# Five PSUM banks in one group, and due offsets by attention unit

## The chip, the cores and the metric

The kernel runs on one core of a Trainium2 chip, as one launch. The metric is the device time in microseconds (us). Before the change the median of three runs is 717.65 us (716.26 to 718.03).

## The reference, cut to what matters

Three stages follow one another on 3072 tokens of 384 features. The first is a linear attention with decay, 4 batches of 768 steps and 8 heads of 48. The second is a feed-forward layer of width 2048. The third is a layer of eight experts of width 1024, of which one is picked for each token.

```python
for t in range(S):                                   # attention, per batch and head
    y[:, :, t] = r_t @ (state + outer(u * k_t, v_t))
    state = w * state + outer(k_t, v_t)
h = x @ w_in                                         # first feed-forward layer
g = where(h >= 1, h, where(h <= -1, 0, (h + 1)**2 / 4))
x = g @ w_out
e = argmax(normed(x) @ normed(emb).T / tau)          # experts
out = gate * (relu(x @ w1[e]) @ w2[e])
```

## The kernel before, in words

Attention is cut into 24 units of 128 tokens, six to a batch. A unit u has three jobs on TensorE, which the planner calls `s0`, `s1` and `s2`:

- `s0` (`s0_pe`, L598 or L606, tiles `psa`) makes the scores of all heads. It fills two PSUM banks at once. VectorE reads them into the SBUF tile `at` (`s0_ev`, L618, or L621 and L625).
- `s1` (`s1_pe`, L672, tile `psy`) makes the outputs, from the scores and from the state that the unit before has left. It fills one bank, which ScalarE and VectorE split into a high and a low float32r part (`xh`, L730, and `xl`, L736).
- `s2` (`s2_pe`, L697 to L706, tile `pskv`) makes the unit's sum of key times value for the state. It fills one bank, which ScalarE or VectorE reads.

The first layer takes blocks of 512 tokens against 16 slices of 128 columns of `w_in`. A step k is one slice: `h` (`m1_h`, nine matmuls into one bank, tile `psh`), on ScalarE `relu`, `over` and `sqr` (L817, L821, L824), on VectorE `max` (L827), on ScalarE `gh` (L831), on GpSimd `gl` (L836), and on TensorE `o` (L858, L859) and `og` (L861), which add the step to three accumulators `acc0` to `acc2`. The bank of `h` comes free after `max`. The experts use `h2` or, for blocks 1 to 5, four tasks `sm` (`sm_pe`), each with one bank.

PSUM has eight banks here: three accumulators, two with the tag `h` and three with the tag `att`. Tag `h` serves the first layer's products, the experts' products, the first two of the four `sm` banks and the diagonal sums of the first four units (`dg_pe`). Tag `att` serves `psa`, `psy`, `pskv`, the other two `sm` banks, the fourth output of the experts and some small tiles.

The order of the work is not written by hand. `Schedule.add` collects tasks with an engine, a duration, dependences, buffers and a due time; `Schedule.run` plays the engines forward. On each engine it takes, among the tasks that can start first, the one due first, and a task whose buffer tag has no free slot has to wait. The slot it finds is the bank the code then uses (`spot`). The due time is moved by the table `SHIFT`, which is looked up under the task's kind (`s0`), its item (`u7`) and both together (`s0_u7`). Before `first_o`, the first task that opens the accumulators, the loop that emits the code fills planned gaps of TensorE with matmuls into a dummy tile (`keep_warm`, L743, tile `wu`). Each engine, and the DMA queue of SyncE, gets its instructions in the planned order.

Of the kernel before, what the change touches and what calls it, by code (L numbers as in the profile page):

```python
# [21 lines left out]
B, H, S, D = 4, 8, 768, 48  # L22
# [204 lines left out]
def d_pe(n):  # L227
    return n / 2300 + 0.011


SHIFT = {"": 62, "az": 0.25, "b0": 147.25, "b2": -0.25, "b4": 29, "b5": 16.75, "dd": 39.25, "dp": -2.25, "dv": 15.5,
# [15 lines left out]
         -6.25, "le0": 7.75, "le1": 46, "le2": -8.75, "lka": -1.5, "lkl": -25.5, "lkm": 6.75, "look": 6, "max":  # L247
# [5 lines left out]
         "smc1": 60.25, "sqa": 2.25, "sqr": 95.25, "sqs": 22.5, "swd": 70.5, "swl": 27, "sws0": 25.5, "sws1": -10.25,  # L253
# [7 lines left out]
         "wb2": 29.75, "wb3": -386.25, "whi": -13, "whp": -29.75, "wkc": 27, "wkd": 28.75, "wkr": -10.5, "wl": 47,  # L261
         "wlo": -0.25, "wlp": -88.75, "wp1": 7.5, "wp2": 3, "wp3": -29, "x1ld": -13, "x1st": -35.75, "x2h": 120.5,
         "x2l": 15.25, "x2ld": -25.5, "xth0": 88.75, "xth1": -7, "xtl0": -3, "xtl1": -35.25, "xts0": -50, "xts1":
         -61.25, "xts2": -25.25, "xts3": -16.25}
U_DVE, U_PE, W_DVE = 4.7, 3.5, 4.0
# [5 lines left out]
def fused_kernel(ctx, tc, att, wcol, wrow, ub, ucol, win, wout, emb, tau, w1, w2, out):  # L271
# [28 lines left out]
    now, turn = {}, {}  # L300

    def spot(tag, bufs):
        if now.get(tag):
            return f"{tag}{now[tag].pop(0)}"
        assert "all" not in now, tag
        turn[tag] = turn.get(tag, -1) + 1
        return f"{tag}{turn[tag] % bufs}"

# [174 lines left out]
    n = 1  # L483
# [73 lines left out]
    def dg_pe(u):  # L557
        s = st[u]
        s["dgp"] = psum("h", [128, H], "psdg", 2)
        for p in range(NP):  # L560
            nc.tensor.matmul(s["dgp"][:, 2 * p:2 * p + 2], lhsT=s["kr"][:, p, :], rhs=uw[:, p, :], start=True, stop=True)
# [245 lines left out]
    def m1_h(m, f, c0, n, f0=0, f1=NF):  # L807
        xh, xl = xT[m]
        hp = psum("h", [128, 512], "psh", 2)[:, :n]
        for kk in range(KD):  # L810
            prod3(hp, win_h[:, kk, f * 128:(f + 1) * 128], win_l[:, kk, f * 128:(f + 1) * 128],
                  xh[:, kk, c0:c0 + n], xl[:, kk, c0:c0 + n], kk == 0, kk == KD - 1)
        return hp
# [327 lines left out]
    def sm_pe(b, q, i, ws):  # L1141

        p = psum("h" if i < 2 else "att", [128, 2, 256], f"psm{i}", 2 if i < 2 else 3)
        mq[b, q, i] = p
# [44 lines left out]
    def m2_hpe(b, f, ws):  # L1189
        n = blocks2[b][1]  # L1190
        _, xh, xl = x2[b][:3]
        hp = psum("h", [128, 512], "psh2", 2)[:, :n]
        for kk in range(KD):
            prod3(hp, ws[0][:, kk, f * 128:(f + 1) * 128], ws[1][:, kk, f * 128:(f + 1) * 128],
                  xh[:, kk, :n], xl[:, kk, :n], kk == 0, kk == KD - 1)
        return hp
# [51 lines left out]
    def m2_store(b, i, o):  # L1248
# [3 lines left out]

    sch = Schedule({"att": 3, "h": 2, "acc0": 1, "acc1": 1, "acc2": 1, "ld": 4, "attn": 2, "x1": 2, "xh": 2, "xl": 2,
                    "a": 2, "gh": 3, "gl": 3, "ru": 1, "dg": 2, "dv": 1, "at0": 1, "at1": 1, "state": 2, "kk": 2, "hw": 2, "gate": 1},
# [40 lines left out]
    def go(k):  # L1295
        return [seq[k]] if seq.get(k) else []
    for m in range(len(blocks1)):
        xbuf[m] = Buf("xh"), Buf("xl")
    for u in range(NU):
# [31 lines left out]
        if u < RAMP:  # L1331
            dpb = Buf("h")
            kr = add("kr", f"u{u}", "Pool", 1.5, lambda u=u: prep_kr(u), [rk], due - 6.5, alloc=[rub], use=[ab])
# [85 lines left out]
    for k, s in enumerate(steps):  # L1419
        m, f, c0, n, f0, f1 = s  # L1420
        hb, ab, ghb, glb = Buf("h"), Buf("a"), Buf("gh"), Buf("gl")
        toks = [u for u in range(NU) if unit_blk[u][0] == m and c0 <= unit_blk[u][1] < c0 + n]
        h = add("h", f"k{k}", "PE", 9 * d_pe(n), run(("h", k), m1_h, *s[:4]), [w_ready["in", f // 2], prev_h] + [lo_of[u] for u in toks],
                T[k], alloc=[hb], use=list(xbuf[m]))
        prev_h = h_of[k] = h
        r = add("relu", f"k{k}", "ACT", 0.65, lambda k=k, n=n: got.update({("a", k): m1_relu(got["h", k], n)}), [h], T[k], alloc=[ab], use=[hb])
        q = add("over", f"k{k}", "ACT", 0.65, lambda k=k: m1_over(got["a", k]), [r], T[k], use=[ab])
# [138 lines left out]
    for k, (b, f) in enumerate(steps2):  # L1566
# [40 lines left out]
        if b in SB:  # L1607
            if f % 2 == 0:
                q = f // 2
                mb = [Buf(x) for x in ("h", "h", "att", "att")]  # L1610
                gb2 = [(Buf("gh"), Buf("gl")) for _ in range(2)]
# [23 lines left out]
        if b not in SB:  # L1635
            hb, ghb, glb = Buf("h"), Buf("gh"), Buf("gl")
            h = add("h2", f"b{b}", "PE", 9 * d_pe(n), lambda b=b, f=f: got.update({("h2", b, f): m2_hpe(b, f, ws)}),
                    his + los + [w2_ready[f // 2], prev_h], due, alloc=[hb], use=[xhb, xlb])
            prev_h = h
            if f in (0, 5):  # L1640
                p2_go[f // 5] = h
            g = add("gh2", f"b{b}", "ACT", d_act(n), lambda b=b, f=f: got.update({("g2", b, f): m2_gh(b, f, got["h2", b, f])}), [h], due, alloc=[ghb], use=[hb])
            g2 = add("gl2", f"b{b}", "DVE", d_dve(n), lambda b=b, f=f: m2_gl(b, f, got["h2", b, f], got["g2", b, f]), [g], due, alloc=[glb], use=[hb, ghb])
# [271 lines left out]
```

## Time and profile before

| | |
|---|---|
| median of three runs | 717.65 us |
| the profiled execution's own time | 718.3 us |
| its span, first to last instruction | 716.6 us |
| PE busy (TensorE) | 705.6 us, 98% |
| DVE busy (VectorE) | 444.2 us, 62% |
| ACT busy (ScalarE) | 413.4 us, 58% |
| POOL busy (GpSimd) | 299.7 us, 42% |
| granted TensorE clock | 0.999 of full speed |

The trace is one execution on the chip. A timeline row gives the start, the time covered, the engine, the line of the kernel, the operation, output and inputs, the number of instructions merged and, in brackets, how long the engine sat idle before the row and what ended that. Matmuls overlap in the pipe: one of 128x512 is shown with 0.40 us and the next begins 0.23 us after it, so the distance between two starts is what it costs. The busy time of PE therefore covers short gaps too.

### The profile page before, as it was taken

The page shows a single profiled execution, that of the slowest core. Times are in us where ns is not written, and L with a number is a line of the kernel's source. Part 1 is how long each engine was busy: PE and PEld are TensorE (multiplying, and loading weights), DVE is VectorE, ACT ScalarE, POOL GpSimd, SP SyncE. Part 2 cuts the span into 40 slices and gives each one's busy share as a digit, 9 for nine tenths or more (in the row PEclk, how much of TensorE's full clock was granted, in tenths as well). Part 3 has the DMA queues.
Part 4 walks back from the last instruction along what each step waited for, and adds up shares of the span by engine and source line. Part 5 has one row for each costly group of instructions (what it writes and reads, how often), then busy time and mean ns, then how long its engine had stood idle before and what let it go on. Part 6 is the DMA issues. An engine that isn't in the chain of part 4 may idle for free.

```text
span 716.6 us, 14161 instructions
## 1 busy us (share of the span) xinstructions
PE 705.6 (98%) x5727; PEld 596.4 (83%) x5727; DVE 444.2 (62%) x824; ACT 413.4 (58%) x738; POOL 299.7 (42%) x247
## 2 busy tenths in 40 slices
PE   8999999999999999999999999999999999999997
PEld 7788887877777888777778878888789999999996
DVE  7988787777777614925274444321657886848952
ACT  3366667674546555745667868776536455437431
POOL 5599965645646633453233313334452113012000
PEclk9999999999999999999999999999999999999999
DMA  8666535222513402510046545300412111102011
GB/s 301 218 224 213 182 132 183 90 97 88 194 67 131 140 12 71 202 31 1 1 143 238 192 138 166 95 0 1 132 45 67 54 57 45 46 22 68 1 45 48
DMA packets 26136, 74.93 MB, mean 105 GB/s; under 512 B 2505, under 2 KB 9682, under 8 KB 26066
## 3 DMA queue, kind: packets, MB, share of 16 engines
q1 hardware_dynamic: 25778, 73.59, 30.4%
q8 instruction: 46, 0.75, 0.4%
q10 hardware_dynamic: 288, 0.39, 0.1%
q14 instruction: 24, 0.20, 0.1%
HBM read 62.74 MB, written 11.01 MB: 103 GB/s over the span
## 4 chain that ended last, share of the span: by engine, by line
PE 82%; DVE 9%; ACT 3%; issue 2%; POOL 2%; DMA 1%; DVEq 0%; ACTq 0%; SPq 0%; POOLq 0%
PE psh L323 9%; PE psh L325 8%; PE psh L324 8%; PE acc L861 8%; PE acc L858 8%; PE acc L859 8%; PE o L1228 5%; PE o L1225 4%; PE o L1226 4%; PE psm L323 3%; PE psm L324 3%; PE psm L325 3%; PE psy L672 3%; DVE a L827 1%; PE psa L606 1%
## 5 line engine op out<-in xcount | busy, mean ns | idle before, releaser
L836 POOL TENSOR_TENSOR gl<-a,gh 128x512 fp32r<-128x512 f32 (+1 forms) x98 | 139.4, 1425 | 183.3 <-ACT gh L831 175.4
L827 DVE TENSOR_TENSOR a<-psh,a 128x512 f32<-128x512 f32 (+1 forms) x98 | 66.3, 677 | 138.4 <-ACT a L824 136.9
L323 PE MATMUL psh<-xh,win_h 128*128 128x512 f32 (+1 forms) x294 | 117.6, 400 | 0.8 <-DVE a L827 0.8
L817 ACT ACTIVATE a<-psh,half 128x512 f32<-128x512 f32 (+1 forms) x98 | 66.2, 675 | 88.5 <-PE psh L325 68.4
L858 PE MATMUL acc<-gh,wout_h 128*128 128x512 f32 (+1 forms) x294 | 115.6, 394 | 0.2 <-ACT gh L831 0.2
L325 PE MATMUL psh<-xh,win_l 128*128 128x512 f32 (+1 forms) x294 | 114.9, 391 | 0.0
L324 PE MATMUL psh<-xl,win_h 128*128 128x512 f32 (+1 forms) x294 | 114.8, 391 | 0.0
L859 PE MATMUL acc<-gh,wout_l 128*128 128x512 f32 (+1 forms) x294 | 114.5, 391 | 0.0
L831 ACT ACTIVATE gh<-a 128x512 fp32r<-128x512 f32 (+1 forms) x98 | 60.5, 619 | 49.3 <-DVE a L827 45.4
L861 PE MATMUL acc<-gl,wout_h 128*128 128x512 f32 (+1 forms) x294 | 82.1, 392 | 1.1 <-POOL gl L836 1.1
L1185 DVE TENSOR_TENSOR sc<-sc,psm 128x256 f32<-128x256 f32 x160 | 59.2, 416 | 17.3 <-ACT sc L1175 11.3
L323 PEld LDWEIGHTS psh<-xh,win_h 128*128 128x128 f32 x294 | 55.2, 188 | 16.5 <-DVE a L827 2.7
L858 PEld LDWEIGHTS acc<-gh,wout_h 128*128 128x128 f32 x294 | 55.2, 188 | 14.0 <-ACT gh L831 0.6
L861 PEld LDWEIGHTS acc<-gl,wout_h 128*128 128x128 f32 x294 | 54.0, 188 | 14.9 <-POOL gl L836 2.3
L325 PEld LDWEIGHTS psh<-xh,win_l 128*128 128x128 f32 x294 | 55.2, 188 | 12.8
L859 PEld LDWEIGHTS acc<-gh,wout_l 128*128 128x128 f32 x294 | 55.3, 188 | 12.4
L1225 PE MATMUL o<-w2h,gh 128*128 128x384 f32 x192 | 64.9, 338 | 0.0
L324 PEld LDWEIGHTS psh<-xl,win_h 128*128 128x128 f32 x294 | 55.3, 188 | 11.3
L1226 PE MATMUL o<-w2l,gh 128*128 128x384 f32 x192 | 64.4, 336 | 0.0
L821 ACT ACTIVATE a<-a 128x512 f32<-128x512 f32 (+1 forms) x98 | 60.8, 621 | 2.4
L824 ACT ACTIVATE a<-a 128x512 f32<-128x512 f32 (+1 forms) x98 | 60.6, 618 | 2.0
L1200 ACT ACTIVATE gh<-sc 128x512 fp32r<-128x512 f32 x40 | 24.5, 627 | 43.2 <-DVE sc L1185 30.7
(216 smaller groups left out, 1372.2 us busy)
## 6 DMA issues: line engine op xcount, KB each, us to landing
att<-att SPq DMA_DIRECT2D x22, 736.0 KB, 4.6
w<-wout SPq DMA_DIRECT2D x16, 768.0 KB, 4.4
w<-win SPq DMA_DIRECT2D x16, 768.0 KB, 5.3
attn<-att SPq DMA_DIRECT2D x20, 384.0 KB, 3.5
x1d<-x SPq DMA_DIRECT2D x6, 768.0 KB, 4.7
x1f<-x1d SPq DMA_DIRECT2D x6, 768.0 KB, 4.8
out<-o SPq DMA_DIRECT2D x10, 384.0 KB, 2.4
hw<-w SPq DMA_DIRECT2D x8, 384.0 KB, 3.6
```

The source lines that it names most:

```text
L323: nc.tensor.matmul(o, lhsT=sh, rhs=mh, start=first, stop=False, skip_group_check=True)
L324: nc.tensor.matmul(o, lhsT=sh, rhs=ml, start=False, stop=False, skip_group_check=True)
L325: nc.tensor.matmul(o, lhsT=sl, rhs=mh, start=False, stop=last, skip_group_check=True)
L817: nc.scalar.activation(out=a, in_=hp, func=AF.Relu, bias=half[:, 0:1], scale=0.5)
L821: nc.scalar.activation(out=a, in_=a, func=AF.Relu, bias=1.0, scale=-1.0)
L827: nc.vector.tensor_tensor(out=a if out is None else out, in0=hp, in1=a, op=ALU.max)
L836: (eng or nc.gpsimd).tensor_tensor(out=gl, in0=a, in1=gh.bitcast(F32), op=ALU.subtract)
L858: nc.tensor.matmul(o, lhsT=wh, rhs=gh, start=(f == f0 and c0 == 0), stop=False, skip_group_check=True)
L859: nc.tensor.matmul(o, lhsT=wl, rhs=gh, start=False, stop=False, skip_group_check=True)
L861: nc.tensor.matmul(o, lhsT=wh, rhs=gl, start=False, stop=(f == f1 - 1), skip_group_check=True)
L1225: nc.tensor.matmul(o, lhsT=gh[:, c], rhs=ws[2][:, f, :], start=(f == 0), stop=False, skip_group_check=True)
L1226: nc.tensor.matmul(o, lhsT=gh[:, c], rhs=ws[3][:, f, :], start=False, stop=False, skip_group_check=True)
```

## The change

The two banks `h` and the three banks `att` become one group of five with the tag `att`; the planner gives a bank of it to whichever task asks. `relu` tasks get a fixed order, each after the one before. The table `SHIFT` is replaced as a whole; the new one also has entries that move `s0`, `s1` and `s2` of single units. `spot` counts its turns by tag and number of buffers, for the code outside the plan. Nothing is computed otherwise, and no tile changes its size.

```diff
-SHIFT = {"": 62, "az": 0.25, "b0": 147.25, "b2": -0.25, "b4": 29, "b5": 16.75, "dd": 39.25, "dp": -2.25, "dv": 15.5,
...
+SHIFT = {"": -54, "az": -68.5, "b0": -144.75, "b1": -92.5, "b2": -72.5, "b3": -73.75, "b4": -0.5, "b5": 11.5, "dd":
...
+         230, "rt0": -6.25, "rt1": 50, "rt2": 44.25, "ru0": -16.25, "ru1": 159.75, "s0_u0": 15.25, "s0_u1": 177.75,
+         "s0_u10": 17.75, "s0_u11": 81.5, "s0_u12": -1.75, "s0_u13": 76.5, "s0_u14": 0.75, "s0_u15": -24.75,
...
@@ spot
-        turn[tag] = turn.get(tag, -1) + 1
-        return f"{tag}{turn[tag] % bufs}"
+        turn[tag, bufs] = turn.get((tag, bufs), -1) + 1
+        return f"{tag}{turn[tag, bufs] % bufs + (2 if (tag, bufs) == ('att', 3) else 0)}"
@@ dg_pe
-        s["dgp"] = psum("h", [128, H], "psdg", 2)
+        s["dgp"] = psum("att", [128, H], "psdg", 2)
@@ m1_h
-        hp = psum("h", [128, 512], "psh", 2)[:, :n]
+        hp = psum("att", [128, 512], "psh", 2)[:, :n]
@@ sm_pe
-        p = psum("h" if i < 2 else "att", [128, 2, 256], f"psm{i}", 2 if i < 2 else 3)
+        p = psum("att", [128, 2, 256], f"psm{i}", 3)
@@ m2_hpe
-        hp = psum("h", [128, 512], "psh2", 2)[:, :n]
+        hp = psum("att", [128, 512], "psh2", 2)[:, :n]
@@ fused_kernel
-    sch = Schedule({"att": 3, "h": 2, "acc0": 1, "acc1": 1, "acc2": 1, "ld": 4, "attn": 2, "x1": 2, "xh": 2, "xl": 2,
+    sch = Schedule({"att": 5, "acc0": 1, "acc1": 1, "acc2": 1, "ld": 4, "attn": 2, "x1": 2, "xh": 2, "xl": 2,
...
-            dpb = Buf("h")
+            dpb = Buf("att")
...
-        hb, ab, ghb, glb = Buf("h"), Buf("a"), Buf("gh"), Buf("gl")
+        hb, ab, ghb, glb = Buf("att"), Buf("a"), Buf("gh"), Buf("gl")
...
-        r = add("relu", f"k{k}", "ACT", 0.65, lambda k=k, n=n: got.update({("a", k): m1_relu(got["h", k], n)}), [h], T[k], alloc=[ab], use=[hb])
+        r = add("relu", f"k{k}", "ACT", 0.65, lambda k=k, n=n: got.update({("a", k): m1_relu(got["h", k], n)}), [h], T[k], alloc=[ab], use=[hb],
+                after=go("relu"))
+        seq["relu"] = r
...
-                mb = [Buf(x) for x in ("h", "h", "att", "att")]
+                mb = [Buf("att") for _ in range(4)]
...
-            hb, ghb, glb = Buf("h"), Buf("gh"), Buf("gl")
+            hb, ghb, glb = Buf("att"), Buf("gh"), Buf("gl")
```

## Rows read from the trace of the kernel before

**Rows 1.** The page: busy time and share by engine; then PE by slices.

```profile
PE 705.6 (98%) x5727; PEld 596.4 (83%) x5727; DVE 444.2 (62%) x824; ACT 413.4 (58%) x738; POOL 299.7 (42%) x247
PE   8999999999999999999999999999999999999997
```

**Rows 2.** Waits of PE: line, releaser, us in total, times, longest.

```profile
PE wu L743 <- POOL mask L468: 2.0, 1, 2.0
PE acc L861 <- POOL gl L836: 1.1, 2, 0.9
PE psh L323 <- DVE a L827: 0.8, 3, 0.4
PE o L1228 <- DVE gl L1205: 0.6, 1, 0.6
PE psa L598 <- DVE at L618: 0.6, 1, 0.6
```

**Rows 3.** Windows: length, busy by engine (instructions), clock, DMA share, GB/s.

```profile
2.02:36.10 34.08, 33.35 (x471) 27.40 (x471) 30.34 (x61) 9.97 (x30) 18.12 (x21) 1.00 0.79 275
60.00:100.00 40.00, 40.00 (x222) 32.22 (x221) 33.48 (x35) 28.35 (x48) 34.24 (x23) 1.00 0.52 178
150.00:200.00 50.00, 48.42 (x636) 37.67 (x635) 37.39 (x82) 28.89 (x59) 29.00 (x23) 1.00 0.40 133
```

**Rows 4.** Timeline of PE about a trip with scores alone, the first.

```profile
204.27 0.40 PE L324 MATMUL psh<-xl,win_h 128*128 128x512 f32 x1
204.50 0.39 PE L325 MATMUL psh<-xh,win_l 128*128 128x512 f32 x1
204.82 0.90 PE L606 MATMUL psa<-att 64*64 64x128 f32 x32
205.65 0.50 PE L858 MATMUL acc<-gh,wout_h 128*128 128x512 f32 x1
205.98 0.39 PE L859 MATMUL acc<-gh,wout_l 128*128 128x512 f32 x1
```

**Rows 5.** Timeline of PE: the last of the trips with scores alone.

```profile
370.53 0.90 PE L606 MATMUL psa<-att 64*64 64x128 f32 x32
```

**Rows 6.** Timeline of PE: a state sum and scores in one trip.

```profile
150.45 0.54 PE L706 MATMUL pskv<-att,kk 128*32 128x48 f32 x32
150.92 0.90 PE L606 MATMUL psa<-att 64*64 64x128 f32 x32
151.76 0.50 PE L323 MATMUL psh<-xh,win_h 128*128 128x512 f32 x1
```

**Rows 7.** Timeline of PE: a state sum that ends a trip.

```profile
282.55 0.52 PE L706 MATMUL pskv<-att,kk 128*32 128x48 f32 x32
283.01 0.50 PE L323 MATMUL psh<-xh,win_h 128*128 128x512 f32 x1
```

**Rows 8.** Timeline of PE: a product that waits for its bank.

```profile
180.16 0.40 PE L325 MATMUL psh<-xh,win_l 128*128 128x512 f32 x1
180.97 0.50 PE L323 MATMUL psh<-xh,win_h 128*128 128x512 f32 x1 [0.41 <-DVE a L827]
```

**Rows 9.** Lines of PE from 2 to 36.1 us: busy, mean ns, idle before.

```profile
L743 PE MATMUL wu<-mask,ident 128*128 128x128 f32 x44 | 7.2, 329 | 2.0 <-POOL mask L468 2.0
```

**Rows 10.** Timeline of the start, PE about 30 us.

```profile
28.70 1.83 PE L743 MATMUL wu<-mask,ident 128*128 128x128 f32 x14
30.45 0.48 PE L598 MATMUL psa<-att 64*128 64x128 f32 x2
...
31.53 1.16 PE L598 MATMUL psa<-att 64*128 64x128 f32 x14 [0.59 <-DVE at L618]
```

**Rows 11.** Timeline: a unit's scores filled, and the second bank of them read.

```profile
39.35 1.16 PE L598 MATMUL psa<-att 64*128 64x128 f32 x16
...
44.19 0.68 DVE L618 TENSOR_TENSOR at<-psa,mask 128x512 f32<-128x512 f32 x1
```

**Rows 12.** Waits of DVE from 0 to 60 us.

```profile
DVE att L523 <- DMA att<-att: 2.8, 3, 1.4
```

More of the change, by code (lines that the diff above doesn't have):

```diff
@@ L228, in d_pe @@
     return n / 2300 + 0.011
-SHIFT = {"": 62, "az": 0.25, "b0": 147.25, "b2": -0.25, "b4": 29, "b5": 16.75, "dd": 39.25, "dp": -2.25, "dv": 15.5,
[15 rows of a table removed]
-         -6.25, "le0": 7.75, "le1": 46, "le2": -8.75, "lka": -1.5, "lkl": -25.5, "lkm": 6.75, "look": 6, "max":
[5 rows of a table removed]
-         "smc1": 60.25, "sqa": 2.25, "sqr": 95.25, "sqs": 22.5, "swd": 70.5, "swl": 27, "sws0": 25.5, "sws1": -10.25,
[7 rows of a table removed]
[L261 to L264, printed above, removed]
+SHIFT = {"": -54, "az": -68.5, "b0": -144.75, "b1": -92.5, "b2": -72.5, "b3": -73.75, "b4": -0.5, "b5": 11.5, "dd":
[15 rows of a table added]
+         64.25, "le0": 2.5, "le1": 18.5, "le2": -32, "lka": -6.75, "lkl": 0.5, "lkm": -54.5, "look": -78.25, "max":
[14 rows of a table added]
+         "sqa": -18, "sqr": -189.5, "sqs": 24.75, "swd": -6.5, "swh": 8.25, "swl": 46.75, "sws0": -20.25, "sws1":
[11 rows of a table added]
 U_DVE, U_PE, W_DVE = 4.7, 3.5, 4.0
```

65 rows, old and new, of the table SHIFT are left out of this document.

## The prediction

> **What bounds the kernel now.** First the page's busy times and slices: PE is busy 705.6 of 716.6 us and no slice but the first and the last is below nine tenths [rows 1]. No other engine has over 62%. So time can only go where PE does something that is not work, and the view to read next is the waits of PE [rows 2]: 2.0 us before its first matmul, 1.1 for `gl` of GpSimd, 0.8 in three waits of `psh` for `max` on VectorE, 0.6 for `gl` in the experts, 0.6 in one wait of `psa`. Two of these five are waits for a PSUM bank: `max` is the last reader of an `h` bank, and L618 the reader of a `psa` bank. Together 1.4 us. The rest of PE's waste is not idle time and is read from the distances between starts in the timeline. It has two kinds: edges, where PE leaves the long matmuls for small attention ones and comes back, and the dummy matmuls `wu` of the start.
>
> **An edge's price.** In a run of long products the starts are 0.23 us apart. Before a trip the last one takes 204.50 to 204.82 = 0.32, and after it the first takes 205.65 to 205.98 = 0.33 [rows 4]. So a trip costs 0.09 + 0.10 = 0.19 us beside its own work. Eleven trips, from 204.82 to 370.53 us, hold the 32 matmuls of one `s0` and nothing else [rows 4, 5]. That fits three `att` banks: `s0` takes two at once, so scores and both other jobs of a unit do not fit side by side.
>
> **The start.** From 2.02 us to the first product at 36.10 us PE works through attention alone, and VectorE is busy 30.34 of these 34.08 us, 89% [rows 3]. 44 dummy matmuls cover 7.2 us of PE [rows 9]. Nine stand ahead of the plan; the other 35, 35/44 x 7.2 = 5.7 us, are gaps that the plan had. 14 of them stand just before a `psa` that then waits 0.59 us for L618 [rows 10].
>
> **The change part by part.** No matmul, activation, vector operation or transfer is added or taken away, apart from the number of `wu`. All of the effect is order.
>
> 1. *Fewer trips.* With five banks the scores of one unit (two), outputs and state sum of another (one each) and a product (one) fit at once, and offsets by unit can put them next to each other. What a merge is worth: `s2` followed by `s0` takes 150.45 to 150.92 to 151.76, 0.47 + 0.84 us [rows 6]; `s2` at the end of a trip takes 0.46 [rows 7], `s0` alone 0.83 [rows 4]. Inside, a merge costs or saves nothing, so it saves one trip's 0.19. I take six of the eleven lone `s0` as merged: 6 x 0.19 = 1.1 us. Bounds: all eleven, 2.1 us; or six more trips than now, 1.1 us lost, since offsets by unit can also pull jobs apart.
>
>  The edges can be held against a rule. The trace shows 0.09 and 0.10 us at the change from 128*128 to 64*64 and back [rows 4]. The Trainium skill ("TensorEngine Tiling (Array Packing)", Tiling Modes, Key Properties) says that changing the tiling mode, as against the tile, drains the engine. By that rule a merge of scores (64*64) with the other jobs (128*32) still has a change inside, and of four changes only one goes: half a trip's price, 0.1 us, and six merges would give 0.6 us. The row shows no such rest inside [rows 6, 7], as the change into `psa` costs no more than the way out that it replaces; the sum keeps 0.19.
>
> 2. *The waits for a bank.* The three waits of `psh` go if a fourth or fifth bank is free: its inputs are there, only the bank is late. 0.8 us [rows 2]. What is late next is `a`, with two buffers, but ScalarE waits on that, not PE. The wait of `psa` of 0.6 us in the start goes also, but VectorE, at 89%, reads those scores no sooner, so that half comes back later: 0.3. Bounds: nothing, or 1.4 us.
>
> 3. *The start's fill.* The 14 `wu` at 28.70 to 30.45 us, 1.75 us, stand where `s0` could have gone with two more banks [rows 10]. Half of it I count as gained, 0.9 us; the other half returns because VectorE sets the pace. Bounds: nothing, or all planned gaps but a rest, some 4 of 5.7 us. On the other side, loads move too in SyncE's order: VectorE already waits 2.8 us in three waits for attention's inputs [rows 12], with the DMA engines 79% busy there [rows 3]; one more such wait of the longest kind costs 1.4 us.
>
> 4. *Products ahead of `gl`.* The two waits for `gl`, 1.1 us, are GpSimd's lateness, not a bank's. Products that may run further ahead put more PE work between `gh` and `og`, so I count half, 0.5. Bounds: 1.7 us gained with the wait in the experts [rows 2], or as much lost, since the new table reorders GpSimd as well.
>
> 5. *`relu` in order.* ScalarE has 42% idle [rows 1], and the products come in order already; nothing either way. If a `relu` that could run had to wait for an earlier one, that is one wait like those of `psh`, 0.4 us [rows 2].
>
> 6. *The experts.* They have five banks in sum before and after: four `sm` and the fourth output. Their one PE wait is for `gl`, not a bank [rows 2]. Nothing; 0.6 us either side, that wait's size. Changes in `spot` touch only code beside the plan, of which the trace has no rows: nothing.
>
> Sum: 1.1 + 0.8 + 0.3 + 0.9 + 0.5 = 3.6 us. The profiled execution takes 718.3 us, 1.7 over its span; 718.3 - 3.6 = 714.7. It lies 0.65 above the median of the runs, 717.65, so the forecast for a median is **714.1 us**. By the rule in part 1 it would be 714.6.
>
> **The rivals.**
>
> *A. Nothing that can be measured (716.9).* All bank waits that the trace shows are 1.4 us [rows 2], and PE has 98% [rows 1]. If the lone `s0` stand alone because VectorE needs up to 5.5 us to read their banks [rows 11], and not for want of a bank, five banks leave the trips as they are, and the change doesn't do what it says. Then the 0.8 us of the `psh` waits remain: 717.65 - 0.8 = 716.9. Against it: scores, outputs and state sum of a unit fill four banks, which three could not hold whatever VectorE did.
>
> *B. Attention takes the products' banks (721).* Before, two banks were kept for `h`. Now scores can hold theirs for long: begun at 39.35, the second bank read at 44.19 to 44.87, 5.5 us [rows 11]. Two units' scores hold four of the five. A product that then finds no bank waits as at 180.97: the two starts stand 0.81 us apart in place of 0.23, 0.58 lost, of which 0.41 is shown as idle [rows 8]. I take the 0.41, as the other two such waits were shorter [rows 2]. The place is 36 to 200 us, where VectorE has 75 to 84% [rows 3] and is slow to read. One such wait in each of 17 units is 7.0 us; less the 3.6 gained, 717.65 + 3.4 = 721.0. It loses all of the gain from nine waits on (9 x 0.41 = 3.7). For it: a planner that takes the earliest start will fill free banks with scores. Against it: the planner sees the banks, and a product that is due may also go first.
>
> *C. The start comes in (710.5).* If scores run far enough ahead that 4 of the 5.7 us of planned gaps go, with all eleven merges (2.1) and the 1.4 us of bank waits, the sum is 7.5 and the time 717.65 - 7.5 = 710.2; with a small loss elsewhere 710.5. Against it: VectorE's 89% in the start.
>
> **How the numbers follow.** What a measurement of this kernel can tell from no change is about 0.3%, 2.15 us: 715.5 to 719.8. My forecast 0.44, A 0.24, B 0.17, C 0.15. The forecast's own range is 712.7 to 715.9, from parts 1 and 2 at their upper bounds (2.1 + 1.4 + 0.9 + 0.5 = 4.9 gained) to half of the sum (1.8); 0.40 of its 0.44 is below 715.5. Faster: 0.40 + C 0.15 + 0.05 of A = 0.60. Slower: 0.15 of B and 0.02 of A = 0.17. The same: 0.23. The range from 709.5 to 720.2 holds the forecast, A, nearly all of C and the lower tail of B; it leaves out 0.15 above and 0.04 below.
>
> **What would show it.** In the timeline of PE, fewer lone rows of `psa` x32 between long products, and trips in which `psa`, `psy` and `pskv` follow one another. In the waits of PE, `psh <- DVE a` and `psa <- DVE at` gone or under 0.3 us. Fewer than 44 `wu`, and the first `psh` before 35 us. B would show as waits of `psh` for readers of `psa` or `psy`. The prediction is wrong if the number of trips is the same and the time is still lower, or if PE's waits grow over 5.6 us, or if VectorE's idle time between 0 and 60 us grows by waits for transfers.

## The result, and the profile after

The change made the kernel slower: 722.79 us median (722.62 to 723.26, four runs), beside 717.84 for the kernel before in the same session, a ratio of 1.0075 with an interval of 1.0057 to 1.0092. The forecast was 714.1, and the range ended at 720.2. The profiled execution took 722.69 us, its span is 721.0, 4.4 longer. Lines of the changed kernel lie 9 further down at most places.

The page, busy times and PE by slices, as [rows 1]: TensorE does less (10 matmuls, all `wu`), VectorE does the same 824 instructions in 7.6 us more.

```profile
PE 703.3 (98%) x5717; PEld 596.9 (83%) x5717; DVE 451.8 (63%) x824; ACT 413.7 (57%) x738; POOL 297.9 (41%) x247
PE   8899999989999999999999999999999999999997
```

The waits of PE, as [rows 2] (line, releaser, us in total, times, longest). The three waits of `psh` for `max` and the wait of `psa` for L618 are gone. In their place stand waits that the kernel before doesn't have: for `dv`, `at`, `att` and `a` of VectorE. The wait for `gh` of ScalarE, 0.2 us before, is 3.0 now. All waits of PE sum up to 12.2 us, before 5.6.

```profile
PE psy L685 <- DVE dv L596: 3.3, 1, 3.3
PE acc L867 <- ACT gh L840: 3.0, 6, 1.1
PE psh L332 <- DVE at L634: 2.0, 2, 1.8
PE wu L752 <- POOL mask L477: 2.0, 1, 2.0
PE psa L607 <- DVE att L532: 0.5, 1, 0.5
PE pset L794 <- DVE a L836: 0.4, 1, 0.4
PE acc L870 <- POOL gl L845: 0.2, 1, 0.2
```

**The start.** The first product comes at 38.23 us, not at 36.10: 2.13 of the 4.4. TensorE's attention work before it is the same. The timeline of PE and then of VectorE shows where: TensorE waits 3.30 us for `dv`, which VectorE has behind the unpacking of a weight block (L408) whose load came late.

```profile
19.17 0.86 PE L681 MATMUL psy<-att,state 128*32 128x128 f32 x24
...
21.68 0.56 PE L711 MATMUL pskv<-att,kk 128*48 128x48 f32 x16
25.54 0.90 PE L685 MATMUL psy<-ident,dv 128*128 128x128 f32 x3 [3.30 <-DVE dv L596]
26.37 1.51 PE L681 MATMUL psy<-att,state 128*32 128x128 f32 x24
...
38.23 0.37 PE L332 MATMUL psh<-xh,win_h 128*128 128x256 f32 x1
```

```profile
20.08 1.01 DVE L436 SCALAR_TENSOR_TENSOR psw<-w,psw 128x384 uint32<-128x384 uint32 x2
24.60 0.56 DVE L408 TENSOR_SCALAR sc<-w 128x768 uint32<-128x768 uint32 x1 [3.51 <-DMA w<-win]
25.07 0.61 DVE L596 TENSOR_TENSOR dv<-att,psdg 128x256 f32<-128x256 f32 x2
```

Four windows before, in and behind that wait (columns as in [rows 3]; the clock is the figure before the DMA share): busy at full speed, 2.4 GHz; idle; then 3.40 us at 0.50 of it, 1.2 GHz; then full speed again. The 24 matmuls of `psy` at 26.37 take 1.51 us there; at 19.17 the same took 0.86.

```profile
6.00:22.20 16.20, 16.18 (x244) 13.26 (x244) 14.20 (x21) 5.26 (x15) 8.04 (x6) 1.00 0.90 328
...
22.20:25.54 3.34, 0.05 (x3) 0.00 (x1) 0.94 (x3) 1.03 (x4) 0.99 (x1) 1.00 1.00 344
25.54:28.94 3.40, 3.40 (x52) 2.88 (x56) 3.28 (x6) 0.00 (x0) 0.00 (x0) 0.50 0.23 94
28.94:32.00 3.06, 3.06 (x40) 2.31 (x30) 2.05 (x4) 1.22 (x2) 1.27 (x1) 0.99 0.52 127
```

**At 150 us.** The scores of two units in one go (x64) hold four of the five banks; a product then waits 1.80 us for a reader of them, L634, that stands on VectorE behind a copy of 2.21 us and six small table operations (three are shown). PE first, then VectorE, then GpSimd:

```profile
145.62 1.57 PE L615 MATMUL psa<-att 64*64 64x128 f32 x64
...
152.69 0.47 PE L332 MATMUL psh<-xh,win_h 128*128 128x512 f32 x1 [1.80 <-DVE at L634]
```

```profile
146.65 2.21 DVE L644 COPY_PREDICATED at<-sel,dg 128x512 f32<-128x512 int32 x1
148.89 0.35 DVE L768 TENSOR_SCALAR wrc<-mix 1x384 f32<-1x384 f32 x1
149.27 0.55 DVE L770 TENSOR_TENSOR wrc<-wrc,mix 1x384 f32<-1x384 f32 x1
...
151.05 0.54 DVE L779 TENSOR_REDUCE ess<-esq 8x1 f32<-8x384 f32 x1
151.62 0.42 DVE L630 TENSOR_TENSOR at<-psa,sel 128x256 f32<-128x256 f32 x1
151.96 0.58 DVE L634 TENSOR_TENSOR at<-psa,sel 64x128 f32<-64x128 f32 x2
```

```profile
146.42 1.83 POOL L472 TENSOR_TENSOR win_l<-sc,win_h 128x768 fp32r<-128x768 f32 x1
```

From 150 to 200 us VectorE is busy 45.66 us, before 37.39 [rows 3]:

```profile
150.00:200.00 50.00, 46.76 (x573) 36.64 (x572) 45.66 (x94) 24.40 (x49) 26.89 (x23) 1.00 0.39 125
```

**`gh` late.** Six waits of `acc` are for `gh`, which needs `max` of VectorE. At the longest a look at a weight block (L396) stands ahead of `max` (L836), and `acc` waits 1.14 us. VectorE first, then PE:

```profile
371.13 0.94 DVE L396 TENSOR_REDUCE least<-w 128x1 f32<-128x768 f32 x1
372.10 0.69 DVE L836 TENSOR_TENSOR a<-psh,a 128x512 f32<-128x512 f32 x1
...
373.51 0.50 PE L867 MATMUL acc<-gh,wout_h 128*128 128x512 f32 x1 [1.14 <-ACT gh L840]
```

**The sum.** Behind the first product the rows shown hold 5.6 us of waits (3.0 + 2.0 + 0.4 + 0.2), before 2.5 (1.1 + 0.8 + 0.6 in [rows 2]): 3.1 more. Stretches in which TensorE leaves the long matmuls fell from 46 to 40, lone scores among them from 11 to 6: 6 x 0.19 = 1.1 less. That makes 2.0; the last matmul, which ends 4.4 us later, says 4.4 - 2.1 = 2.3. Waits too small for the rows shown (0.2 now, 0.5 before) would make it 1.7, so some 0.3 to 0.6 us aren't accounted for.

### The profile page after: what moved, and what is told of

It reads as the page before. It is cut to its first block, busy times and chain, and to the rows that moved or that the text cites. A ratio compares the mean times of both kernels' runs of the same rounds, so it can differ in the third digit from the quotient of the medians.

```text
span 721.0 us, 14154 instructions
## 1 busy us (share of the span) xinstructions
PE 703.3 (98%) x5717; PEld 596.9 (83%) x5717; DVE 451.8 (63%) x824; ACT 413.7 (57%) x738; POOL 297.9 (41%) x247
## 4 chain that ended last, share of the span: by engine, by line
PE 81%; DVE 10%; DMA 4%; ACT 2%; issue 1%; POOL 1%; SPq 0%; DVEq 0%; ACTq 0%; POOLq 0%
PE psh L332 9%; PE psh L334 9%; PE psh L333 9%; PE acc L867 8%; PE acc L868 8%; PE acc L870 8%; PE o L1234 5%; PE o L1237 5%; PE o L1235 5%; PE psm L332 4%; PE psm L333 4%; PE psm L334 4%; PE psy L681 3%; DMA w<-win 2%; DVE at L644 2%; DMA att<-att 2%
## 5 line engine op out<-in xcount | busy, mean ns | idle before, releaser
L845 POOL TENSOR_TENSOR gl<-a,gh 128x512 fp32r<-128x512 f32 (+1 forms) x98 | 135.9, 1391 | 182.7 <-ACT gh L840 165.5
L836 DVE TENSOR_TENSOR a<-psh,a 128x512 f32<-128x512 f32 (+1 forms) x98 | 66.1, 677 | 150.7 <-ACT a L833 150.2
L332 PE MATMUL psh<-xh,win_h 128*128 128x512 f32 (+1 forms) x294 | 115.6, 393 | 2.2 <-DVE at L634 2.0
```

What stands on the lines that cost most here:

```text
L332: nc.tensor.matmul(o, lhsT=sh, rhs=mh, start=first, stop=False, skip_group_check=True)
L836: nc.vector.tensor_tensor(out=a if out is None else out, in0=hp, in1=a, op=ALU.max)
L845: (eng or nc.gpsimd).tensor_tensor(out=gl, in0=a, in1=gh.bitcast(F32), op=ALU.subtract)
```

## The experiments

Seventeen kernels ran. Times are medians; the ratio is to the kernel before on the same chip in the same session. The change itself has 1.0075. Most kernels change the planned order by a few lines in front of the emitting loop: `find` gives the tasks of that name, `behind` takes tasks out of the order and puts them right behind another.

```diff
-    for task in sch.run():
+    plan = sch.run()
...
+    def find(kind, item):
+        return [t for t in plan if (t.kind, t.item) == (kind, item)]
...
+    def behind(mark, *ts):
...
+        i = plan.index(mark) + 1
+        plan[i:i] = ts
...
+    for task in plan:
```

**Parts of the change: five banks with the old table.** The table of before, everything else of the change.

```diff
-SHIFT = {"": -54, "az": -68.5, ...
+SHIFT = {"": 62, "az": 0.25, ...
```

> One group of five banks and the fixed order of relu, with the table of due offsets of the kernel before. Theory (the time is lost where the new order puts slow VectorE work ahead of what PE waits for, not by the sharing of banks as such): the start has no wait of PE over 1 us, the first product comes at 36 to 37 us, waits of psh for readers of scores stay below 1 us in sum, and the time is 715 to 720.5. Rival 1 (sharing as such: scores take the products' banks): waits of psh for readers of psa or psy of 2 us or more, and 721 or more.

764.7 us, ratio 1.0652 (1.0636 to 1.0668). The theory's number is missed by over 40 us. The rival has the side, but not its sign: `psh` waits only 0.4 us for readers of `psa`. TensorE spends 43.86 us from 186.42 on attention alone, with VectorE busy 40.03 of them and the granted clock at 0.75.

```profile
186.42:230.28 43.86, 27.91 (x729) 23.87 (x728) 40.03 (x82) 8.77 (x26) 21.88 (x18) 0.75 0.53 170
```

**Parts of the change: the new table with two and three banks.** The other edits of the change are taken back, `relu`'s order too.

```diff
-    sch = Schedule({"att": 5, "acc0": 1, ...
+    sch = Schedule({"att": 3, "h": 2, "acc0": 1, ...
```

> Banks split in two and three as in the kernel before, with the new table. Theory (order): the new table still pulls the unpacking of the third weight block ahead on VectorE, PE waits 2 us or more in the start, first product at 37.5 us or later, time 720 or more, though no psh waits for a reader of scores. Rival 1 (sharing): with its two banks back the products don't wait and the time is 718.5 or less.

743.96 us, 1.0388 (1.0361 to 1.0414); nine waits of `psh` for `max`, 10.0 us. The theory has the number, not the reason: TensorE doesn't wait in the start, and the first product comes at 34.95 us, sooner than in either kernel. So neither half of the change gains anything alone: the new table does worse with the split banks than with the shared ones, the old one the other way round.

**Is a table good for one plan only?** The kernel before, each entry of its table moved by up to 2 at random, as

```diff
-SHIFT = {"": 62, "az": 0.25, "b0": 147.25, ...
+SHIFT = {'': 61, 'az': 2.25, 'b0': 145.25, ...
```

> The kernel before with each entry of its table of due offsets moved by a random whole number from -2 to 2 (-2, -1, 0, 1 or 2 us of due time), the banks split as before. Theory (a table fits only the plan it was made for, so the 26 and 47 us of the two mixed kernels tell nothing of the banks): 5 us or more slower than before. Rival 1 (the 47 us of five banks with the old table are the price of sharing): within 3 us of before.

717.96 us, 1.0015 (0.9998 to 1.0031). The theory fell: shifts of 2 us change the order a little and the time not measurably. The 47 us of the first run come with the shared banks (`relu`'s order alone leaves the plan of before as it was). How much of them a table fitted to that split would give back, this run can't say; its shifts are far smaller than what the banks change in the order.

**Attention held to three of the five banks** (old table, as the first run):

```diff
+                if b.tag == "att" and t.kind in ("s0", "s1", "s2", "kkt") and i >= 3:
+                    continue
```

> Five banks in one group, relu order, old table, as in the run that took 764.7, but the planner lets attention (scores, outputs, state sums, transposed keys) have three of the five banks only, so two are left to the products whatever attention does; products may still take all five. Theory (in the run of 764.7 attention swallowed the products' banks): 716 to 721, no trip over 8 us. Rival (what cost 47 us was the products running ahead, or relu in order, or any order that the table was not made for): over 740.

751.36 us, 1.0452 (1.0429 to 1.0475). The theory fell: attention had no bank more than before, and most of the loss, 33 of 47 us, was still there. Two windows show where: all but products alone until 186 us, then some 32 us of attention in which TensorE works 21.85 us, VectorE 28.08.

```profile
100.00:186.00 86.00, 86.00 (x403) 67.93 (x401) 50.88 (x71) 56.09 (x93) 44.02 (x30) 1.00 0.29 95
186.00:218.00 32.00, 21.85 (x517) 18.30 (x517) 28.08 (x61) 5.48 (x16) 14.27 (x12) 0.73 0.48 159
```

A reading of this: with two banks a product had to stop now and then, and attention went in; with five it goes on, and attention comes when it is due all at once, at VectorE's pace. The next two runs put it to the test.

**Products held to two, attention free in all five; and products to three, attention to three, one bank shared.**

```diff
+                if b.tag == "att" and t.kind == "h" and i < 3:
+                    continue
```

```diff
+                if b.tag == "att" and (t.kind == "h" and i < 2 or t.kind in ("s0", "s1", "s2", "kkt") and i >= 3):
+                    continue
```

> Five banks in one group, relu order, old table, as in the run that took 764.7, but the products of the first layer may use two of the five banks only, while attention may use all five. Theory (what broke that order is that products, no longer stopped by two banks, run ahead until attention is due all at once): no trip over 10 us, 717 to 728, at least 20 us below 751.4, the time with attention held to three banks. Rival (any order that the table was not made for is bad, or attention swallows the banks): over 740.

> As the kernel with attention held to three of the five banks (751.4), but the products are held too, to three, so only one bank is shared. Theory (the products' own limit paces attention): one trip of over 15 us is still there, 728 to 748, between that and the kernel with two for the products. Rival (one shared bank is harmless, the loss comes from many): within 3 us of the kernel before.

786.41 us, 1.0966 (1.0927 to 1.1005), and 747.66 us, 1.0433 (1.0396 to 1.047). The first is the worst of all, over the theory's 717 to 728 by 58 us: the limit on the products alone doesn't bring the old time back, and the rival holds there, attention does swallow the banks. 35 waits of `psh` for `max`, every 5.33 us one of 0.86 us, also where VectorE is all but idle (from 250 to 300 us busy 7.71 of 50): scores that nobody reads yet hold one of the two banks (written at 256.38 us, read from 307.62). The waits of PE and two steps of it:

```profile
PE psh L325 <- DVE a L829: 34.5, 35, 2.3
```

```profile
279.41 0.50 PE L325 MATMUL psh<-xh,win_h 128*128 128x512 f32 x1 [0.86 <-DVE a L829]
284.74 0.50 PE L325 MATMUL psh<-xh,win_h 128*128 128x512 f32 x1 [0.86 <-DVE a L829]
```

The second is at the upper end of what was expected, with a stretch of attention of 21.42 us at 187.28. So with the old table sharing costs time from both sides, and one shared bank is enough for 30 us. That the products' limit paces attention fits the long stretches, but no run shows it apart from the table's fit.

**The start: unpack the third weight block later.**

```diff
+    behind(find("wlp", "w1")[0], find("wb1", "w2")[0], find("wb2", "w2")[0], find("wb3", "w2")[0])
```

> The changed kernel with its planned order frozen and one move on VectorE: the three operations that unpack the third weight block (L408, L411, L414) go behind the diagonal term dv of unit 2, the low part of unit 1's outputs and the low part of the second weight block, which then run while VectorE would wait for the block's load. Theory: the wait of PE for dv (3.3 us) is below 0.6, the granted clock stays at 1.00 up to 40 us, the first product comes at 36.1 (35.6 to 36.8) in place of 38.2, and the time is 722.8 - 2.1 = 720.7 (719.8 to 721.6). Rival 2 (VectorE's load in the start sets the pace, wherever the wait stands): PE waits elsewhere in the start, first product at 37.5 or later, gain below 0.8 us.

720.64 us, 1.0041 (1.0028 to 1.0055): 2.15 us gained, as expected. The gain is that of the median; the profiled execution, the slowest of six, doesn't show it. There the load let the unpacking begin at 26.64 us, 2.0 later than in the changed kernel, and `dv` of the next unit stood behind it:

```profile
26.64 0.56 DVE L408 TENSOR_SCALAR sc<-w 128x768 uint32<-128x768 uint32 x1 [3.17 <-DMA w<-win]
...
31.23 0.90 PE L685 MATMUL psy<-ident,dv 128*128 128x128 f32 x3 [3.57 <-DVE dv L596]
```

In the same order with more moves (below) the unpacking began at 24.09, and that wait was 0.3. So the landing of the load decides too; no run moved the load itself.

**The start: the same tasks earlier, with two more.**

```diff
+    behind(find("wlp", "w0")[0], *[find(k, "w2")[0] for k in ("wb1", "wb2", "wb3", "whi", "wlo")])
```

> The changed kernel with its planned order frozen; the five tasks of the third weight block (three unpacking operations on VectorE, the copy on ScalarE, the low part on GpSimd) go behind the low part of the first block, so all of unit 3's scores and the first block's unpacking stand ahead of the wait for that load. Theory (the start loses by what is queued on VectorE behind a late load): no wait of PE over 1 us between 15 and 36 us, clock 1.00 there, first product at 33.5 to 36.5 us in place of 38.2, time 718.5 to 721. Rival 2 (VectorE's load sets the pace wherever the block is unpacked): first product at 37.5 or later, time 721.5 or more.

726.5 us, 1.0131 (1.0116 to 1.0145), against 718.5 to 721 expected. The first product came at 33.04 us, the first `acc` at 42.85, in the changed kernel at 42.58: what was gained in front was waited for right behind, with the clock at half from 39.0 to 45.9. A first product is no measure of a start.

**The start: dummy matmuls in the wait.** Before `s1` of unit 2, a `keep_warm` of 24, which makes 48 instructions, and then one of 13.

```diff
+        if (task.kind, task.item) == ("s1", "u2"):
+            keep_warm(13)
         task.fn()
```

> Kernel after, with 24 dummy matmuls (some 3.0 us) in the 3.3 us in which TensorE waits for dv before the outputs of unit 2; nothing else is moved. Both theories: the granted clock stays at 1.00 from 2 to 40 us, the two psy rows behind the wait take 0.9 and 1.1 us and not 1.5 and 1.7. Theory (VectorE's order sets the pace of the start, the clock is only a follower): the first product comes less than 0.5 us earlier than 38.2, the time is 722.3 to 722.9. Rival (the clock costs what its rows show): the first product at 36.7 to 37.2, the time 721.3 to 721.8.

> Kernel after, with 13 pairs of dummy matmuls (26 instructions, some 3.0 us) in the 3.3 us wait for dv in the start. In the run before this one 24 pairs took 5.6 us and pushed the outputs back by 2.25 us, so it gave no price for the clock. Theory (VectorE's order paces the start, the clock follows): outputs start at 25.3 to 25.6 as in the kernel after, the granted clock stays at 1.00, the first product is less than 0.5 us earlier than 38.2, ratio to the kernel before 1.0065 to 1.0080. Rival (the clock costs what its rows show, 1.2 us): first product at 36.7 to 37.2, ratio 1.0052 to 1.0062.

The first took 5.62 us where 3.3 were free and pushed the outputs to 27.79: 1.0075 (1.0058 to 1.0091), and it gives no price for the clock. The second: 722.05 us, 1.0053 (1.0040 to 1.0066), first product at 36.31, clock 1.00. The rival was right by the ratio, and the first product is even 0.4 before its 36.7 to 37.2. The gain is about 1.6 us by the ratios (0.0022 x 718), whose intervals overlap; the traces say 1.92 for the first product. Of these 0.26 are an earlier load (outputs from 25.28, not 25.54); the other 1.66 are about half of the 3.40 us at half the clock.

```profile
22.27 3.17 PE L752 MATMUL wu<-mask,ident 128*128 128x128 f32 x26
25.28 0.49 PE L685 MATMUL psy<-ident,dv 128*128 128x128 f32 x3
25.70 0.86 PE L681 MATMUL psy<-att,state 128*32 128x128 f32 x24
...
36.31 0.36 PE L332 MATMUL psh<-xh,win_h 128*128 128x256 f32 x1
```

```profile
25.28:28.70 3.42, 3.42 (x79) 2.96 (x78) 3.42 (x7) 1.20 (x2) 0.00 (x0) 1.00 0.42 122
```

**At 150 us: the readers of the scores ahead of the table operations.**

```diff
+    k = plan.index(find("tab0", "")[0])
+    behind(plan[k - 1], find("e0", "u9")[0], find("e1", "u9")[0])
+    behind(find("sqr", "k24")[0], find("tab5", "")[0])
```

> The changed kernel with its planned order frozen and one move near 150 us: VectorE reads the two banks of unit 9's scores before the router's table operations (L768 to L779) and not after them; the square root of that table goes behind sqr of step 24 on ScalarE. Theory: the wait of psh for at (1.8 us near 151 us) is below 0.3 and the time falls by 1.0 to 1.8 us, to 721.0 to 721.8. Rival 2 (VectorE, busy 91% from 150 to 200 us, is the bound there): the wait comes back before the table's transpose or in acc<-gh, and the gain is below 0.5 us.

723.37 us, 1.0088 (1.0068 to 1.0107). The wait of `psh` went (0.2 left), `pset` waits 2.4 us in its place, as the rival said.

**`max` ahead of the long task before it, in five places; and with the start's repair.**

```diff
+    for k, kind, item in (("k2", "wb1", "w3"), ("k5", "wb2", "w6"), ("k30", "rk", "u15"), ("k36", "rk", "u19"), ("k65", "lkm", "look")):
+        behind(find("max", k)[0], find(kind, item)[0])
```

> Kernel after, order kept, but on VectorE five max (steps 2, 5, 30, 36 and 65) go ahead of the one long task that stands directly before them (weight unpacking twice, a product with the decay twice, the look at the scores once). Theory (what the products wait for is the place of max in VectorE's order): the waits of acc for gh fall from 3.0 to under 0.5 us and the time by 2.0 to 2.7, to 720.1 to 720.8. Rival (VectorE is so full there that the task moved back makes the next wait): waits of psh, pset or psa grow by as much, the time is 722.0 to 723.3.

> Kernel after with both repairs: unpacking of the third weight block behind the low part of the second (gave 2.15 us alone), and the five max ahead. Theory (the two are independent): 717.3 to 718.8, the time of the kernel before. Rival (the start's loss and the later waits are one VectorE backlog, and what is gained early is waited for later): 719.8 to 721.0, no better than the first repair alone.

725.53 us, 1.0096 (1.0080 to 1.0111), and 722.59, 1.0068 (1.0049 to 1.0087). Both are slower than even the rivals said, and for another reason: the fifth move took the first look instead of the one before `max`, the looks behind it came late, and `acc` waits 2.9 to 3.0 us for `gh` at 382 to 385 us. Behind it the granted clock is 0.50 for 3.4 us in both. In the second of the two:

```profile
382.45 0.80 PE L867 MATMUL acc<-gh,wout_h 128*128 128x512 f32 x1 [2.91 <-ACT gh L840]
```

With the right look moved:

```diff
+        mark = find("max", k)[0]
+        behind(mark, [t for t in find(kind, item) if plan.index(t) < plan.index(mark)][-1])
```

> Kernel after with the start's repair and max of steps 2, 5, 30, 36 and 65 ahead, as in the run with ratio 1.0068, but now the look moved behind max of step 65 is the last one before it; there the first look had been moved, and a wait of acc of 2.9 us at 382.45 us came with it. Theory (VectorE's order is the cause, wait by wait): that wait is gone and nothing else changes, so 2.9 us less, a ratio of 1.0015 to 1.0035 to the kernel before. Rival (that wait only shows a backlog which comes back elsewhere): a ratio of 1.005 to 1.0075.

719.47 us (twelve runs), 1.0024 (1.0012 to 1.0036). The theory: that wait is gone, and 3.2 us came off (0.0044 x 718). The waits of PE are 9.8 us in all now, `acc` for `gh` 1.8, `dv` 0.3, and the first product starts at 35.10, 1.0 sooner than in the kernel before.

```profile
PE wu L752 <- POOL mask L477: 2.0, 1, 2.0
PE psh L332 <- DVE at L634: 2.0, 2, 1.8
PE acc L867 <- ACT gh L840: 1.8, 5, 0.6
PE psa L607 <- DVE att L532: 1.3, 1, 1.3
...
PE psy L685 <- DVE dv L596: 0.3, 1, 0.3
```

**At 150 us: another bank for the product,** in that kernel. Scores of unit 10 behind it, banks exchanged, VectorE untouched.

```diff
+    s0, k25, k27 = find("s0", "u10")[0], find("h", "k25")[0], find("h", "k27")[0]
...
+    s0.alloc[0].slot, k25.alloc[0].slot, k27.alloc[0].slot = 1, 2, 2
+    behind(k25, s0)
```

> The repaired kernel (ratio 1.0024), and the scores of unit 10 go behind the product that waits 1.80 us near 150 us for a bank of unit 9's, with the two banks exchanged between them; VectorE's order is not touched. Theory (VectorE's backlog at 140 to 156 us sets the pace, whoever holds the banks): that wait goes, and pset, acc or the next psh waits for VectorE instead, together 1.4 to 2.2 us; ratio 1.0018 to 1.0032. Rival (attention's hold on four of five banks is the cause, the rival of the prediction): no such wait comes instead, the wait's 1.8 less one trip's 0.19 are gained, ratio 0.9995 to 1.0008.

721.03 us, 1.0046 (1.0034 to 1.0059): dearer than either expected. The product no longer waits; `pset` and `psy` wait for VectorE, 3.0 us where 0.4 were (0.8 more is `dv` in the start, whose load came later again). From 140 to 156 us VectorE is busy 15.47 of 16.

```profile
153.77 0.35 PE L794 MATMUL pset<-ident,mix 8*128 8x8 f32 x3 [1.57 <-DVE a L836]
...
164.75 0.86 PE L681 MATMUL psy<-att,state 128*32 128x128 f32 x24 [1.48 <-DVE at L634]
```

**Less for VectorE, in both kernels.** Units 8 to 13 lose the second of their two `copy_predicated`.

```diff
     def s0_dg(u, j):
...
+        if j and DIAG <= u < DIAG + 6:
+            return
```

> The changed kernel without one of two copies of the diagonal term into the scores (L644, second half of the heads) for units 8 to 13: six VectorE operations of 0.7 to 2.2 us left out between 146 and 250 us, all else in the same order. Theory (VectorE is the bound there in the changed kernel): 722.8 falls by 1.5 to 4 us, to 718.8 to 721.3, and the waits of acc for gh and of pset shrink. Rival 3 (VectorE is not what PE loses by there): under 0.7 us.

> The kernel before with the same six VectorE operations left out (L635). Theory: there VectorE is busy 76% from 145 to 200 us and PE hardly waits for it, so 717.6 falls by less than 1.0 us. Rival 3: both kernels gain alike.

721.65 us, 1.0069 (1.0053 to 1.0085), and 716.22, 0.9984 (0.9975 to 0.9992). By the ratios the changed kernel gains 0.4 us, which its interval can't tell from nothing, and the kernel before 1.1. The theory's 1.5 to 4 us are missed: less work for VectorE there helps the changed kernel no more than the other, so the sum of that work is not what sets the two apart.

The `relu` order was not run alone: put into the kernel before, it leaves the planned order of every engine as it was. No kernel that does all of the work beat the one before.

## Why the prediction was wrong

The forecast was 3.6 us gained; 5.0 were lost. Two steps failed: the start, which was to gain, lost 2.13, and behind the bank waits stood others of VectorE's making, which the sum put at nothing.

**Part 1, fewer trips, was right** in size: six stretches fewer at 0.19. Part of it came as drawn: from 60 us on scores stand beside outputs or state sums in seven trips, before in three. Part came otherwise: the scores of two units in one stretch, three times, and that is what holds four banks.

**Part 2, bank waits, was right on the names and wrong on what is late next.** Both waits went. The step that failed is "What is late next is `a`, with two buffers, but ScalarE waits on that, not PE." What came next was `gh`, by way of `max` on VectorE: 3.0 us in six places, before 0.2 in one. Moving `max` ahead took 1.2 us of it back: the traces have 3.0 and 1.8, the ratios 1.0041 and 1.0024, with intervals that overlap.

**Part 3, the start, failed** and is the largest term: 0.9 gained was forecast, 2.13 lost measured. The sum counted 14 `wu` as room that PE could use. They went (34 `wu` in place of 44), and the wait for VectorE stood open elsewhere. The new plan had no gap at that place, so no `wu` stood in it when the load was late; the wait of 3.3 us then also took half the clock for 3.4 us. Filled, the first product comes at 36.31, 0.21 from before: the loss is mostly the clock, for which the sum had no term. With the unpacking moved and the five `max` ahead it comes at 35.10: the room that the sum counted was there, and VectorE's order and the clock took it away. The bound of this part held "one more such wait of the longest kind", 1.4 us; VectorE's wait for the load was 3.5. Two of the prediction's own signs of being wrong showed: PE's waits grew by 6.6 us, and VectorE's waits for transfers up to 60 us grew from 5.4 to 7.1.

One reading of this part was wrong besides. The first row of `wu` has 18 of them (nine calls make two each), not nine, so the plan's gaps held 26 of the 44, some 4.3 us (26/44 x 7.2) and not 5.7; the bound of 4 us and rival C are too large by that.

```profile
2.02 3.83 PE L743 MATMUL wu<-mask,ident 128*128 128x128 f32 x18 [2.02 <-POOL mask L468]
```

**Part 4, `gl`:** its waits fell from 1.1 to 0.2 us as half expected, but `acc` now waits a step earlier, for `gh`, which may be why `gl` is in time. **Part 5 held:** no difference. **Part 6** held in its bounds: the experts' wait of 0.6 us for `gl` is gone.

**Rival A** is out, as the trips fell, and **rival C** too, as the start went the other way. **Rival B** had the side and, by chance, the neighbourhood of the number. Its mechanism is real: in the new order it shows once at any size, 1.80 us at 150 us, and not in 17 units (from 36 to 200 us, the place it names, the trace before has the scores of seven). It is not what costs there: given another bank, the product goes and VectorE is waited for elsewhere. In the old order, with the products held to two of the shared banks, it costs 0.86 us a step, twice the 0.41 assumed.

**What the sum lacked as a whole** is a term for VectorE's order. It took the new table as one that fits, and gave a loss only to banks and transfers; yet where VectorE is 75 to 89% busy [rows 3], a long task that its order puts ahead of a short one finds little slack. Of the 5 us, 3.7 came back by moving three unpackings and five long tasks (1.0075 to 1.0024), with all of the work done. The remaining 1.7, all behind the first product, stay open: the wait at 150 us moves when it is taken away, and no run removed it.

## What to carry to other kernels

A limit on buffers may also be a pacer. With the old table every kind of sharing cost some 30 us or more, and the traces show attention in long stretches; that the two banks had let it in a little at a time fits this and isn't shown by itself. Before pooling buffers, ask which work the limit holds back, and what will hold it back then.

On the engine that feeds the bound one, read the order and not only the load: look for a long task, or one that waits for a load, just ahead of a short one that the bound engine needs.

A filler that covers planned gaps covers no others: an unplanned gap costs its own length and can cost the clock behind it. Here it did so behind the wait for `dv` and behind the 2.91 us at 382 us, and not behind the 1.80 us at 150 us.

## What the runs showed of the hardware

TensorE was busy 16.18 of 16.20 us at 2.4 GHz; after 3.34 us with next to no work it ran 3.40 us at 1.2 GHz (the windows above). With 26 dummy matmuls in the gap it stayed at 2.4 GHz. Behind the wait of 1.80 us at 150 us it stayed there, too: the window from 150 to 200 us has 1.00.

The copy at 146.65 us lasts 2.21 us; two of the same form take 1.38 together at 369.86, 0.69 each, with GpSimd idle. It began while GpSimd's L472 ran, which ended at 146.42 + 1.83 = 148.25, and took 0.61 us from there. The same at 63.56 us: an unpacking (L411) of 2.64 us that takes 0.95 at 25.60, beside an L472 from 63.54 to 65.37.

```profile
369.86 1.38 DVE L644 COPY_PREDICATED at<-sel,dg 128x512 f32<-128x512 int32 x2
```

The Trainium skill ("SBUF — State Buffer", section "SBUF: two separate sides") says that VectorE and GpSimd share a pair of ports by an exclusive lock: the one that starts first has it for a whole instruction and the other one waits; for VectorE that holds, among others, for operations with two SBUF inputs, beside a GpSimd operation that reads SBUF. Both cases are such, and both agree: VectorE's operation ends 0.61 and 0.83 us after GpSimd's, a little less than its own length (0.69 and 0.95). So a changed order can make VectorE late with the same work on both: of its 7.6 us more, 4.4 are in the 32 copies (30.8 for 26.4) and 2.6 in the 14 unpackings of L411 (24.3 for 21.7).
